# Threshold attention and a squared-ReLU layer on one core: another order of attention's steps, and chunk loads asked for earlier

## The chip, the cores and the metric

One Trainium2 chip, one of its cores. TensorE (PE) multiplies matrices, VectorE (DVE), ScalarE (ACT) and GpSimd (POOL) work element by element, and SyncE (SP) issues nearly all transfers of this kernel from one queue. Each engine takes its instructions in the order of its own queue and waits on semaphores for the others. The metric is the device time of one execution in microseconds (us), as the median of several runs.

## The reference

The inputs are q, k and v of 8 batches, 8 heads, 576 positions and 64 values per head, a threshold `tau`, and two weights, 512 x 2048 and 2048 x 512. Cut to what matters:

```python
scores = 1 / 8 * np.matmul(q, k.transpose(0, 1, 3, 2))
thresh = np.max(scores, axis=-1, keepdims=True) - tau
scores = np.where(scores >= thresh, scores, -1000000000.0)
scores = scores - np.max(scores, axis=-1, keepdims=True)
attn = np.exp(scores)
attn = attn / (np.sum(attn, axis=-1, keepdims=True) + 1e-09)
x = np.matmul(attn, v)              # then (B, H, S, D) -> (B*S, H*D): 4608 x 512
h = np.maximum(x @ w_in, 0.0)
out = (h * h @ w_out).astype(np.float32)
```

q, k, v and the output are 32-bit floats. The two weights come in as 64-bit floats, so the kernel reads them as pairs of 32-bit words and makes 32-bit floats of them with integer and float operations on the chip ("conversion").

## The kernel before

The kernel has two stages. Attention comes first and leaves its result, transposed, in the tensors `xT`; the two layers follow, each as products of 7 x 7 sums of blocks (a scheme with fewer products and more additions).

**Attention.** Two heads are a pair, 32 pairs in all. Rows of scores are worked in 144 units of 128 rows of two heads; two units, A and B, make a period, so there are 72 periods. For a unit: products of q and k into the PSUM tile `sc` (six banks, L448: `SA`, `SB` for 512 of the 576 columns, `RA`, `RB` for the rest of 64), a copy to SBUF that takes the row minimum of the scores, which are kept with their sign turned (`top`, L466, VectorE, one for each head), the threshold from the minimum (`least`, L473, POOL), the exponential (`pow`, L476, ScalarE), the mask, which multiplies by the comparison with the threshold and sums the row (`mask`, L481, VectorE). For the two units of a period: `over` (L488, POOL) adds 1e-9 to the row sums and `inv` (L491, VectorE) takes the reciprocal. The masked weights are then transposed by TensorE in three fills, `V`, `W`, `U` (L392), which are copied out by ScalarE as `eV`, `eW`, `eU` (L539). `V` and `U` use the one tile of the pool `pt` in turn, `W` uses banks 2 and 3 of `sc`, together with `Q` (L531), which spreads the reciprocals. `PV` (L548) multiplies by v into banks 0 and 5 of `sc`. `x` takes this out: the first head by a ScalarE copy (L679), the second by a VectorE product with the reciprocals (L681); `xm` (L691, POOL) scales the first head in SBUF. While weights are converted, ScalarE copies both heads and POOL scales both. `T` and `eT` (L412, L417, L425) turn q and k of a later pair through banks 1 and 4. A product must wait for every other engine that has touched its bank.

**The order.** It is written by hand. A period's list of names says in which order the steps are put into the queues; a name with dashes is the step of as many periods earlier:

```python
for name in BEGIN_WITH.get(p) or (CONVERTING if converts(p) else PLAIN):
    step(name.rstrip("-"), p - name.count("-"))
```

`CONVERTING` holds while weights are converted (periods 2 to 34), `PLAIN` after that; periods 0 and 1 have lists of their own. Nothing else ties the engines to a period: each runs on in its queue as far as its semaphores let it. A step that was already put in the queue by an earlier period isn't put in again.

**Weights.** The 16 blocks of the first weight and 16 blocks of the second are converted in attention, one chunk a period. `fetch` asks for a chunk's raw words (512 KB, L192) into one of four buffers `raw` of the region `cv`. `c1` (L206, ScalarE) makes a working tile `a`, one of four; `c2` (L213), `c3` (L220) run on POOL, `c4` (L228), `c5` (L236) on VectorE, and `c6` (L246, POOL) adds the parts into the tile `wall`, or, for the second weight, into `a`, which is then stored to HBM (L248). `c1` runs two periods after the `fetch`, `c6` two periods after `c1`. After the last conversion the steps `s1` and `s2` make one sum each of the first weight's blocks, and later of the first x, on POOL (L122 and L125); `s2` ends with period 59.

**Transfers.** `ahead(n)` issues up to n of the waiting loads of q and k (L296, L310, L317, L318; nine for a pair). `give_x` puts the stores of x (L594) in a list, and `ask` issues them; `valued` issues the loads of v (L327). All of these are in SP's queue, in the order in which the steps are called. `xm` calls `ask(False)` and `ahead(2)`, `ahead` at the head of a period issues three, and `c6` issues the store of its chunk at once.

Of the kernel before, what the change touches and what calls it, by code (L numbers as in the profile page):

```python
# [10 lines left out]
FP32 = mybir.dt.float32  # L11
# [37 lines left out]
def kernel(  # L49
# [88 lines left out]
    W_IN, W_OUT = {}, {}  # L138
    wall = ctx.enter_context(tc.tile_pool(name="wp", bufs=1)).tile([P, 49 * BANK], FP32, name="wall")

    def weight_tile(W, m, k):
        at = OUTER.index(m) * 7 + INNER.index(k)
        W[m, k] = wall[:, ds(at * BANK, BANK)]
        return W[m, k]
# [33 lines left out]
    def fetch(m):  # L178
        if m is None or m in asked_for:
            return  # L180
        asked_for.add(m)
        src = chunks[m][3]
        if not is_wide and m < 16:
            nc.sync.dma_start(out=weight(m)[:, :], in_=src)
            return
        raw = cv.tile([P, 2 * WC], I32, tag="raw", bufs=4, name="raw")
        if not is_wide:
            nc.sync.dma_start(out=raw[:, 0:WC].bitcast(FP32).rearrange("p (k o) -> p k o", k=4), in_=src)
            nc.sync.dma_start(out=slot_of(*chunks[m][1:3]), in_=raw[:, 0:WC].bitcast(FP32))
            return  # L190
        three = (lambda t: t.rearrange("p (k o) -> p k o", k=4)) if m >= 16 else (lambda t: t)
        nc.sync.dma_start(out=three(raw[:, :]), in_=src.bitcast(I32))  # L192
        raws[m] = raw
# [7 lines left out]
    def convert1(m):  # L201
        if m not in raws:
            return
        lo, hi = pick(raws[m], 0), pick(raws[m], 1)
        a = cv.tile([P, WC], I32, tag="a", bufs=4, name="a")
        nc.scalar.activation(out=a.bitcast(FP32), in_=hi.bitcast(FP32), func=AF.Abs)  # L206
        parts[m] = (lo, hi, a)
        raws.pop(m)
# [31 lines left out]
    def convert6(m):  # L240
        if m not in parts:
            return
        lo, hi, a = parts.pop(m)
        if m < 16:
            a = weight(m)[:, :].bitcast(I32)
        nc.gpsimd.tensor_tensor(out=a, in0=hi, in1=lo, op=ALU.add)  # L246
        if m >= 16:
            nc.sync.dma_start(out=slot_of(*chunks[m][1:3]), in_=a.bitcast(FP32))  # L248

    def sums(W, which, at):  # L250

# [353 lines left out]
    def begun(n):  # L605
        return starts.get(n)

    FIRST_PERIOD = -2
    PLAIN = """
        ahead PV-- RA- c2- c4- T- W-- U- c5- Q-- c1- maskB0-- x-- eT- SA- xm-- s1 maskB1-- RB- c3- eW-- SB-  # L610
        eU- topA0- V- powA0- eV- topA1- topB0- topB1- powA1- powB0- over- leastA- powB1- inv- c6 maskA0- s2-
        maskA1- leastB- fetch
    """.split()
    CONVERTING = """
        ahead SB- c1 RA topB0- powA1- c2- topB1- PV- c5- powA0- maskA0- eT- leastB- over- V- x- T powB0- SA
        RB W- maskA1- c3 c4 inv- Q- c6- fetch topA0 eV- topA1 leastA U xm- maskB0- powB1- eW- eU maskB1- s1
        s2
    """.split()

    BEGIN_WITH = {  # L620
        0: """
        SA RA RB SB fetch ahead topA0 T topA1 leastA topB0 topB1 leastB powA0 powA1 eT powB0 powB1 maskA0
        maskA1 maskB0 maskB1
        """.split(),
        1: """
        fetch ahead SA RA RB SB T eT over topA0 topA1 leastA inv V topB0 topB1 leastB powA0 powA1 eV W Q
        powB0 eW maskA0 maskA1 powB1 maskB0 maskB1 next
        """.split(),
    }

# [6 lines left out]
    def period(p):  # L637
# [34 lines left out]
        def values_out():  # L672
            if not has(2 * m):
                return
            late["x"] = x = sb.tile([P, 2, P], FP32, tag="x", bufs=2, name="x")
            for j in range(2):
                from_ = sc[:, ds(5 * j * BANK, P)]
                if converts(p) or j == 0:
                    made = nc.scalar.copy(x[:, j, :], from_)  # L679
                else:  # L680
                    made = nc.vector.tensor_tensor(  # L681
                        out=x[:, j, :], in0=from_, in1=wT[m][:, ts(SCALE_AT + j, P)], op=ALU.mult
                    )
                touch("x", made, 5 * j * BANK, P, m)

        def given_out():
            if has(2 * m):
                x = late.pop("x")
                made = x[:, 0 : 1 + converts(p), :].rearrange("p j n -> p (j n)")
                scale = wT[m][:, ds(SCALE_AT * P, (1 + converts(p)) * P)]  # L690
                nc.gpsimd.tensor_tensor(out=made, in0=made, in1=scale, op=ALU.mult)  # L691
                wT.pop(m)
                valued(m)
                give_x(m, x)
            ask(False)
            ahead(2)

        def scored(n):
            if has(n):
# [7 lines left out]
        def every(key):  # L707
# [10 lines left out]
            "c1": lambda: convert1(begun(p)), "c2": lambda: convert2(begun(p)),  # L718
            "c3": lambda: convert3(begun(p)), "c4": lambda: convert4(begun(p - 1)),
            "c5": lambda: convert5(begun(p - 1)), "c6": lambda: convert6(begun(p - 1)),  # L720
            "s1": lambda: sums_due(p) and sums_step(), "s2": lambda: sums_due(p) and p < 60 and sums_step(), "ahead": lambda: ahead(3 if p > 1 else 4),
            "fetch": lambda: fetch(begun(p + 2)),
            "next": lambda: fetch(begun(p + 3)),
        }
        steps["over"] = lambda: do(a, "over")
        steps["inv"] = lambda: do(a, "inverse")
# [654 lines left out]
```

## Time and profile before

| | |
|---|---|
| median of 3 runs | 1304.61 us (1299.85 to 1307.76) |
| the profiled execution | 1303.65 us, with a span of 1301.5 us |
| granted TensorE clock, mean | 0.995 |
| busy share of the span | PE 98%, PEld 86%, DVE 76%, POOL 76%, ACT 65% |
| SP's queue (q1) | 192.87 MB, 51.2% of the 16 DMA engines |

Times in the views count from the start of the span. PE is the matmuls, PEld their weight loads, SPq the issue of transfers by SP. A line number is that of the kernel before; a row gives the engine, the line, the operation, and what is written from what. "<-" names who ended the wait ahead of an instruction, inferred from semaphores. The ends of matmuls are modelled. Attention fills the first 512 us of the span: the first product of the layers begins at 512.11.

### The profile page before, as it was taken

The page shows a single profiled execution, that of the slowest core. Times are in us where ns is not written, and L with a number is a line of the kernel's source. Part 1 is how long each engine was busy: PE and PEld are TensorE (multiplying, and loading weights), DVE is VectorE, ACT ScalarE, POOL GpSimd, SP SyncE. Part 2 cuts the span into 40 slices and gives each one's busy share as a digit, 9 for nine tenths or more (in the row PEclk, how much of TensorE's full clock was granted, in tenths as well). Part 3 has the DMA queues.
Part 4 walks back from the last instruction along what each step waited for, and adds up shares of the span by engine and source line. Part 5 has one row for each costly group of instructions (what it writes and reads, how often), then busy time and mean ns, then how long its engine had stood idle before and what let it go on. Part 6 is the DMA issues. An engine that isn't in the chain of part 4 may idle for free.

```text
span 1301.5 us, 46003 instructions
## 1 busy us (share of the span) xinstructions
PE 1275.3 (98%) x18287; PEld 1118.3 (86%) x18287; DVE 989.4 (76%) x2384; ACT 847.9 (65%) x1537; POOL 989.4 (76%) x1070
## 2 busy tenths in 40 slices
PE   7999999999999999999999999999999999999998
PEld 4777767777777777988888888999999999999998
DVE  5999999999999995786886878867646654665463
ACT  5999989998898985566665866675523432343240
POOL 2999988877777531898987998868777767777775
PEclk8999999999999999999999999999999999999999
DMA  6565566544333312567768868679645224522511
GB/s 161 139 171 155 145 185 187 154 103 101 85 77 80 80 41 56 179 201 198 222 182 223 226 173 235 179 279 376 232 158 163 84 84 159 163 74 91 162 34 34
DMA packets 291414, 196.21 MB, mean 151 GB/s; under 512 B 100096, under 2 KB 252160, under 8 KB 291200
## 3 DMA queue, kind: packets, MB, share of 16 engines
q1 hardware_dynamic: 289888, 192.87, 51.2%
q8 instruction: 144, 2.36, 0.8%
q14 instruction: 70, 0.57, 0.1%
q10 hardware_dynamic: 1312, 0.41, 0.1%
HBM read 120.85 MB, written 72.35 MB: 148 GB/s over the span
## 4 chain that ended last, share of the span: by engine, by line
PE 83%; ACT 8%; DMA 3%; issue 2%; POOL 2%; SPq 1%; DVE 1%; ACTq 0%; DVEq 0%; POOLq 0%
PE po L1112 29%; PE ph L970 15%; PE sc L548 11%; PE sc L448 10%; PE ph L977 10%; PE pt L392 4%; ACT arena L539 3%; ACT arena L476 2%; PE sc L531 1%; PE sc L412 1%; DMA arena<-in_q_dram 1%; DVE arena L125 1%; POOL arena L125 1%; DMA arena<-xT 1%; ACT c L826 1%
## 5 line engine op out<-in xcount | busy, mean ns | idle before, releaser
L125 POOL TENSOR_TENSOR arena<-arena 128x512 f32<-128x512 f32 (+1 forms) x314 | 378.1, 1222 | 135.4 <-DVE arena L125 112.4
L1112 PE MATMUL po<-wall,arena 128*128 128x128 f32 x3528 | 394.7, 275 | 1.4 <-ACT arena L787 1.4
L1112 PEld LDWEIGHTS po<-wall,arena 128*128 128x128 f32 x3528 | 394.2, 192 | 1.8 <-ACT arena L787 1.8
L125 DVE TENSOR_TENSOR arena<-ph,arena 128x512 f32<-128x512 f32 x378 | 255.0, 688 | 79.8 <-PE ph L970 29.5
L122 POOL TENSOR_TENSOR arena<-arena 128x128 f32<-128x128 f32 (+1 forms) x322 | 270.0, 840 | 25.3 <-DMA arena<-w 9.4
L970 PE MATMUL ph<-arena,wall 128*128 128x256 f32 x1176 | 256.2, 380 | 1.9 <-DVE arena L125 1.6
L970 PEld LDWEIGHTS ph<-arena,wall 128*128 128x128 f32 x1176 | 222.3, 190 | 35.6 <-DVE arena L125 5.7
L125 DVE TENSOR_TENSOR arena<-po,arena 128x128 f32<-128x128 f32 x378 | 108.1, 289 | 168.6 <-PE po L1112 164.4
L476 ACT ACTIVATE arena<-arena 128x576 f32<-128x576 f32 x288 | 213.1, 779 | 24.2 <-DVE arena L466 24.2
L466 DVE TENSOR_SCALAR_CACHE_REDUCE arena<-sc 128x576 f32<-128x576 f32 x288 | 203.3, 752 | 31.5 <-issue 12.6
L481 DVE SCALAR_TENSOR_TENSOR arena<-arena 128x576 f32<-128x576 f32 x288 | 225.7, 820 | 1.3 <-ACT arena L476 1.3
L826 ACT COPY c<-arena 128x512 f32<-128x512 f32 (+1 forms) x295 | 169.0, 578 | 71.6 <-DVE arena L122 35.8
L448 PE MATMUL sc<-arena 64*64 64x512 f32 (+1 forms) x2304 | 191.8, 417 | 7.1 <-ACT arena L679 1.9
L548 PE MATMUL sc<-arena 64*64 64x128 f32 (+1 forms) x5760 | 164.7, 262 | 0.7 <-ACT arena L539 0.7
L122 DVE TENSOR_TENSOR arena<-arena,c 128x512 f32<-128x512 f32 x235 | 154.2, 665 | 11.0 <-ACT c L826 9.0
L548 PEld LDWEIGHTS sc<-arena 64*64 64x64 f32 x5760 | 149.9, 134 | 3.6 <-ACT arena L539 0.9
L539 ACT COPY arena<-pt 128x1024 f32<-128x1024 f32 x144 | 147.1, 1022 | 6.9 <-PE pt L392 6.3
L448 PEld LDWEIGHTS sc<-arena 64*64 64x64 f32 x2304 | 88.6, 134 | 73.1 <-issue 44.4
L473 POOL TENSOR_SCALAR arena<-arena,tau_p 128x2 f32<-128x2 f32 x144 | 84.7, 588 | 78.2 <-DVE arena L466 57.0
L787 ACT COPY arena<-po 128x128 f32<-128x128 f32 x63 | 16.6, 264 | 186.7 <-PE po L1112 183.9
L977 PE MATMUL ph<-arena,wall 128*128 128x128 f32 x1176 | 132.0, 275 | 0.6 <-DVE arena L681 0.6
L977 PEld LDWEIGHTS ph<-arena,wall 128*128 128x128 f32 x1176 | 131.6, 192 | 0.9 <-issue 0.7
(54 smaller groups left out, 1141.9 us busy)
## 6 DMA issues: line engine op xcount, KB each, us to landing
arena<-g SPq DMA_DIRECT2D x144, 256.0 KB, 4.5
g<-arena SPq DMA_DIRECT2D x192, 128.0 KB, 3.0
w<-arena SPq DMA_DIRECT2D x60, 256.0 KB, 2.8
wall<-w SPq DMA_DIRECT2D x49, 256.0 KB, 5.3
g<-arena SPq DMA_DIRECT2D x48, 256.0 KB, 3.7
arena<-w SPq DMA_DIRECT2D x44, 256.0 KB, 3.3
arena<-in_v_dram SPq DMA_DIRECT2D x32, 288.0 KB, 4.2
out_dram<-arena SPq DMA_DIRECT2D x70, 128.0 KB, 2.2
```

Of the source, the lines that this page charges most:

```text
L122: e.tensor_tensor(out=out, in0=x, in1=y, op=ALU.subtract)
L125: e.tensor_tensor(out=out, in0=x, in1=y, op=ALU.add)
L448: made = nc.tensor.matmul(sc[at, ds(to, count)], lhs, kT[rows, ds(at_k, count)], start=True, stop=True)
L466: made = nc.vector.tensor_scalar(out=s[:, j, :], in0=sc[:, ds(at, S)], scalar1=1.0, scalar2=None, op0=ALU.mult, op1=ALU.min, accum_out=nmx ...
L476: nc.scalar.activation(out=w[:, :, j, :], in_=of(j), func=AF.Exp, bias=nmx[:, j : j + 1], scale=-1.0)
L481: nc.vector.scalar_tensor_tensor(out=w[:, :, j, :], in0=of(j), scalar=thr[:, j : j + 1], in1=w[:, :, j, :], op0=ALU.is_le, op1=ALU.mult, a ...
L539: touch("weights", nc.scalar.copy(joined(to), whole(pt, 0, count)), at, 2 * BANK, m)
L548: made = nc.tensor.matmul(sc[ds(u * D, D), ds(5 * j * BANK + row, count)], loaded_v[i][rows, (c - (u != j)) % CH, :], wT[m][rows, ds(weigh ...
L826: nc.scalar.copy(c, y)
L970: nc.tensor.matmul(to[:, 2 * j : 2 * j + 2, :], W_IN[m, k][:, ts(2 * h + j, P)], part_x(steps, k, m), start=(not more and j == 0), stop=Tr ...
L977: nc.tensor.matmul(to[:, j, :], W_IN[m, k][:, ts(j, P)], x, start=(not more and j == 0), stop=True, skip_group_check=True,)
L1112: nc.tensor.matmul(to, g[:, j, :], w[:, j, :], start=(not more and j == 0), stop=(j == 3), skip_group_check=True)
```

## The change

Only attention's code is touched. The list for periods without conversions has another order, with some steps of an earlier period than before. In both lists the steps `put`, `give`, `fetch` and `ahead` stand together at the head: `put` issues the stores of chunks that `c6` has queued up to then, `give` the stores of x, `fetch` asks for the chunk that is used three periods later (and for the one two periods later, if it hasn't been asked for), `ahead` issues five loads. `c6` and `xm` no longer issue transfers, but for the loads of v. The raw words have seven buffers, in the last two of the seven rows of `wall`, which hold no block until the sums are made; `a` has six, and x three. The lists of periods 0 and 1 place `fetch` and `ahead` otherwise.

```diff
+    raw_places = Region(wall, OUTER.index(5) * 7 * BANK, 49 * BANK)
...
-        raw = cv.tile([P, 2 * WC], I32, tag="raw", bufs=4, name="raw")
+        raw = raw_places.tile([P, 2 * WC], I32, tag="raw", bufs=7, name="raw")
...
-        a = cv.tile([P, WC], I32, tag="a", bufs=4, name="a")
+        a = cv.tile([P, WC], I32, tag="a", bufs=6, name="a")
...
         if m >= 16:
-            nc.sync.dma_start(out=slot_of(*chunks[m][1:3]), in_=a.bitcast(FP32))
+            made_chunks.append((slot_of(*chunks[m][1:3]), a.bitcast(FP32)))
+
+    made_chunks = deque()
+
+    def put():
+
+        while made_chunks:
+            to, from_ = made_chunks.popleft()
+            nc.sync.dma_start(out=to, in_=from_)
...
     PLAIN = """
-        ahead PV-- RA- c2- c4- T- W-- U- c5- Q-- c1- maskB0-- x-- eT- SA- xm-- s1 maskB1-- RB- c3- eW-- SB-
-        eU- topA0- V- powA0- eV- topA1- topB0- topB1- powA1- powB0- over- leastA- powB1- inv- c6 maskA0- s2-
-        maskA1- leastB- fetch
+        put give fetch ahead eU-- powA0-- V-- powA1-- eV-- maskA1-- PV-- powB1-- c1- RA- powB0-- T--
+        maskA0-- U- W-- Q-- x-- c4- maskB1-- SA- eT-- RB- maskB0-- topA0- over- topA1- c2 s2 leastA- eW--
+        SB- topB0- s1- c5 c6 topB1- inv- leastB- xm-- c3
     """.split()
     CONVERTING = """
-        ahead SB- c1 RA topB0- powA1- c2- topB1- PV- c5- powA0- maskA0- eT- leastB- over- V- x- T powB0- SA
-        RB W- maskA1- c3 c4 inv- Q- c6- fetch topA0 eV- topA1 leastA U xm- maskB0- powB1- eW- eU maskB1- s1
-        s2
+        put give fetch ahead SB- c1 RA topB0- powA1- c2- topB1- PV- c5- powA0- maskA0- eT- leastB- over- V-
+        x- T powB0- SA RB W- maskA1- c3 c4 inv- Q- c6- topA0 eV- topA1 leastA U xm- maskB0- powB1- eW- eU
+        maskB1- s1 s2
     """.split()
     BEGIN_WITH = {
         0: """
-        SA RA RB SB fetch ahead topA0 T topA1 leastA topB0 topB1 leastB powA0 powA1 eT powB0 powB1 maskA0
+        fetch SA RA RB SB topA0 T ahead topA1 leastA topB0 topB1 leastB powA0 powA1 eT powB0 powB1 maskA0
         maskA1 maskB0 maskB1
         """.split(),
         1: """
-        fetch ahead SA RA RB SB T eT over topA0 topA1 leastA inv V topB0 topB1 leastB powA0 powA1 eV W Q
-        powB0 eW maskA0 maskA1 powB1 maskB0 maskB1 next
+        fetch ahead SA RA RB SB T ahead eT over topA0 topA1 leastA inv V topB0 topB1 leastB powA0 powA1 eV W
+        Q powB0 eW maskA0 maskA1 powB1 maskB0 maskB1
         """.split(),
     }
...
-            late["x"] = x = sb.tile([P, 2, P], FP32, tag="x", bufs=2, name="x")
+            late["x"] = x = sb.tile([P, 2, P], FP32, tag="x", bufs=3, name="x")
...
                 give_x(m, x)
-            ask(False)
-            ahead(2)
...
-            "s1": lambda: sums_due(p) and sums_step(), "s2": lambda: sums_due(p) and p < 60 and sums_step(), "ahead": lambda: ahead(3 if p > 1 else 4),
-            "fetch": lambda: fetch(begun(p + 2)),
-            "next": lambda: fetch(begun(p + 3)),
+            "s1": lambda: sums_due(p) and sums_step(), "s2": lambda: sums_due(p) and p < 60 and sums_step(), "ahead": lambda: ahead(5),
+            "fetch": lambda: (fetch(begun(p + 2)), fetch(begun(p + 3)) if p > 1 else None), "put": put, "give": lambda: ask(False),
```

## The prediction

> **What bounds the kernel now.** I read the page's chain of waits first, then the busy time by stretch around one line, then the timeline of one steady period, then the waits of the stage with conversions.
>
> ```profile
> PE 83%; ACT 8%; DMA 3%; issue 2%; POOL 2%; SPq 1%; DVE 1%; ACTq 0%; DVEq 0%; POOLq 0%
> ```
>
> ```profile
> core 0: us, DVE busy (x), PEclk, DMA share, GB/s
> 44.17:91.85 47.68, 1.11 (x7) 1.00 0.60 160
> 91.85:248.15 156.30, 3.48 (x22) 0.99 0.62 168
> 161.03:170.86 9.83, 0.16 (x1) 0.92 0.78 218
> 266.46:426.68 160.22, 4.15 (x24) 1.00 0.39 90
> 426.68:499.00 72.32, 1.90 (x11) 1.00 0.25 57
> ```
>
> The chain is mostly TensorE, but the change touches attention alone, so its stages must be read by themselves. The second view counts the reciprocal of the softmax sums, one in each period; every stretch starts and ends just ahead of one. Attention runs at four speeds: 47.68/7 = 6.81 us a period with conversions in a quiet stretch, 156.30/22 = 7.10 in the rest of the conversions (one period took 9.83), 160.22/24 = 6.68 without conversions, and 72.32/11 = 6.57 at the end, where POOL makes one weight sum a period instead of two.
>
> One period without conversions, in the timeline (start, length, engine, line; in brackets the idle time before and who ended it):
>
> ```profile
> 403.96 0.76 DVE L466 TENSOR_SCALAR_CACHE_REDUCE arena<-sc 128x576 f32<-128x576 f32 x1 [0.56 <-issue]
> ...
> 404.71 0.58 PEld L392 LDWEIGHTS pt<-ident,arena 64*128 64x128 f32 x16 [0.81 <-ACT arena L539]
> ...
> 404.76 0.78 ACT L476 ACTIVATE arena<-arena 128x576 f32<-128x576 f32 x1 [0.62 <-DVE arena L466]
> ...
> 405.50 0.29 POOL L473 TENSOR_SCALAR arena<-arena,tau_p 128x2 f32<-128x2 f32 x1 [0.64 <-DVE arena L466]
> 405.52 1.01 ACT L539 COPY arena<-pt 128x1024 f32<-128x1024 f32 x1
> ...
> 405.76 1.28 POOL L122 TENSOR_TENSOR arena<-arena 128x512 f32<-128x512 f32 x1
> ...
> 406.68 0.17 DVE L491 RECIPROCAL arena<-arena 128x4 f32<-128x4 f32 x1
> ...
> 407.01 0.80 POOL L473 TENSOR_SCALAR arena<-arena,tau_p 128x2 f32<-128x2 f32 x1
> ...
> 408.13 0.58 PEld L392 LDWEIGHTS pt<-ident,arena 64*128 64x128 f32 x16
> ...
> 408.32 0.81 DVE L481 SCALAR_TENSOR_TENSOR arena<-arena 128x576 f32<-128x576 f32 x1
> ...
> 409.05 2.39 PE L448 MATMUL sc<-arena 64*64 64x512 f32 x24
> ...
> 409.06 0.28 DVE L681 TENSOR_TENSOR arena<-sc,arena 128x128 f32<-128x128 f32 x1
> ...
> 409.26 0.80 DVE L481 SCALAR_TENSOR_TENSOR arena<-arena 128x576 f32<-128x576 f32 x1
> 409.37 0.61 ACT L539 COPY arena<-sc 128x512 f32<-128x512 f32 x1
> 409.39 0.30 PEld L448 LDWEIGHTS sc<-arena 64*64 64x64 f32 x6 [0.20 <-DVE arena L681]
> 409.41 1.79 POOL L122 TENSOR_TENSOR arena<-arena 128x512 f32<-128x512 f32 x1
> ...
> 409.84 1.06 ACT L539 COPY arena<-pt 128x1024 f32<-128x1024 f32 x1
> ...
> 410.63 0.76 DVE L466 TENSOR_SCALAR_CACHE_REDUCE arena<-sc 128x576 f32<-128x576 f32 x1 [0.56 <-issue]
> ...
> 411.29 0.23 POOL L488 TENSOR_SCALAR arena<-arena 128x4 f32<-128x4 f32 x1
> ...
> 411.38 0.33 PEld L392 LDWEIGHTS pt<-ident,arena 64*128 64x128 f32 x8 [0.81 <-ACT arena L539]
> ```
>
> VectorE idles 0.56 us ahead of its first row minimum (L466, 403.96 and 410.63); it is dense for 6.67 - 0.56 = 6.11. What holds it stands further up. The scores (L448) start at 409.05, but the half that writes the second head's bank can't start until VectorE has scaled the second head's output out of that bank (L681, 409.06 to 409.34): weight loads resume at 409.39, with that instruction named. From L681's end to the next row minimum is 410.63 - 409.34 = 1.29 us, in which VectorE has one mask (L481) left, 0.74 from start to start (408.32 to 409.06). The rest is the idle time. So the loop that sets the period is VectorE, L681, the second half of the scores, the scores' rests, VectorE. TensorE loses 409.39 - 409.05 = 0.34 us in it.
>
> **The order without conversions.** In each engine's own queue the change is smaller than the list of names suggests, since most names only turn round in the loop. What is left: L681 goes ahead of both masks of the second unit instead of between them; masks and exponentials swap heads; the copy eV goes behind a second exponential; the fills U and W swap; and POOL runs over, sum, leastA, sum, leastB, scaling of x, where one sum stood behind the scaling of x.
>
> Step by step. With L681 one mask earlier, two masks (1.48 us) cover the 1.29, and VectorE need not idle there. TensorE then starts both halves together: its period is 6.67 - 0.34 = 6.33. That is more than VectorE's 6.11, so TensorE becomes the limit. ScalarE is idle 0.62 ahead of 404.76, so it needs 6.05; its last copy (eU) ends at 410.90, 0.48 ahead of the next fill at 411.38. The copy eV ends at 406.53; one exponential (0.78) later it still ends 0.8 ahead of the fill U at 408.13, which reuses its buffer; beyond that cover it would cost TensorE one for one. The swap of U and W moves work within TensorE's queue, ahead of the sums' spread as before, and costs nothing. I take 6.35 for both kinds of period: 24 x (6.68 - 6.35) + 11 x (6.57 - 6.35) = 7.9 + 2.4 = 10.3 us gained. The smallest gain is none; a middle one is the time that the waits view gives to L681 alone, 7.2 us in 35 periods:
>
> ```profile
> PEld pt L392 <- ACT arena L539: 28.4, 35, 0.8
> ...
> PEld sc L448 <- DVE arena L681: 7.2, 26, 0.5
> ```
>
> I stay near 0.34, because the loads' wait leaves out the time in which the first half's loads went on alone. The largest gain is VectorE's own density: 35 x 0.56 = 19.6.
>
> The first of these rows seems to promise more: TensorE waits 0.8 us a period for the copy eU. But eU has ended 0.48 us earlier, and the fill starts as the scores' last product ends (409.05 + 2.39 = 411.44, an end that is modelled). I count that row as the drain of the scores and give nothing for it. If the releaser that the view names were the right one, the period could fall to VectorE's 6.11, the second rival. The Trainium skill, "TensorEngine Tiling (Array Packing)", section "Tiling Modes", says that a change of tiling mode drains the array; here scores use 64*64 tiles and fills 64*128. By that rule the 0.8 us stays whatever ScalarE does, against what the view's releaser says.
>
> **Chunks, buffers and stores.** The transfers are the same in number and size, and the conversions stay. What moves is SP's queue: the store of a finished chunk and the two or three stores of x go to the start of the next period, where POOL has mostly made them; the chunk load is asked for three periods ahead and, with seven buffers in the idle end of the weight tile, waits for no POOL addition; five loads of q and k follow in one place.
>
> ```profile
> SPq L594 <- POOL arena L691: 23.6, 17, 3.9
> SPq L192 <- POOL wall L246: 5.8, 6, 2.0
> ```
>
> ```profile
> ACT arena L206 <- DMA arena<-in_moe_w_out_dram: 2.5, 3, 1.7
> ```
>
> ```profile
> 157.44 2.13 SPq L296 DMA_DIRECT2D arena<-in_q_dram  x2
> ...
> 160.22 0.38 SPq L192 DMA_DIRECT2D arena<-in_moe_w_out_dram  x1
> ...
> 160.31 0.34 PE L412 MATMUL sc<-ident,arena 64*128 64x64 f32 x2 [0.37 <-DMA arena<-in_q_dram]
> ...
> 165.94 0.69 ACT L206 ACTIVATE arena<-arena 128x512 f32<-128x512 f32 x1 [1.74 <-DMA arena<-in_moe_w_out_dram]
> ```
>
> SP stands still 23.6 us behind x and 5.8 behind chunks, so loads come late. The chunk asked for at 160.22 is needed at 165.94, after a wait of 1.74 us; exponentials and row minima queue behind it, and that period is the one of 9.83, 3.0 over the quiet 6.81. q asked for at 157.44 is waited for at 160.31. All excess over the quiet pace is 156.30 - 22 x 6.81 = 6.5 us. With a lead of three periods (20 us instead of 5.7) the chunk's part goes; of the other 3.5 I give about half to late q and k: 4.5 us gained, between 0 and 6.5. The quiet pace stays: the change takes nothing off VectorE. SP still waits for the scaling of x once a period, with the chunk load and five loads behind it; their lead covers that (the first rival, if not). The later stores keep x and a chunk's working tile one period longer, which the third and the sixth buffer cover; without them the copies of x (L679, L681) would wait.
>
> The start may lose. A second chunk load in one place and one more now stand ahead of the last loads of the third pair's k.
>
> ```profile
> 19.77 1.26 SPq L310 DMA_DIRECT2D arena<-in_k_dram  x2
> ...
> 29.08 0.47 PE L412 MATMUL sc<-ident,arena 64*128 64x64 f32 x10
> ```
>
> ```profile
> arena<-in_moe_w_out_dram SPq DMA_DIRECT2D x16, 512.0 KB, 5.0
> ```
>
> ```profile
> 15.00:20.00 5.00, 1.77 (x44) 1.29 (x42) 5.00 (x16) 4.34 (x7) 1.32 (x3) 0.91 1.03 317
> ```
>
> Two chunks of 512 KB at 317 GB/s are 3.3 us. Those k loads were issued from 19.77 on and turned at 29.08; SP no longer waits in between, so I take 0.5 us lost, with bounds 3.3 lost and 1 gained.
>
> **Sum.** 10.3 + 4.5 - 0.5 = 14.3 us off the profiled execution's 1303.65, which is 1.0 under the median of the runs, 1304.61: 1289.4 by the profile, 1290 as a median. The layers behind attention are the same instructions.
>
> **Rivals.**
> - Slower, by late loads: chunk loads now go ahead of q and k in SP's queue. If q and k land as late as at 160.31, each turn (L412) waits for a chunk's passage, 512 KB at 317 GB/s = 1.65 us. TensorE has 6.81 - 6.33 = 0.48 to spare, so 1.2 us in each of the 29 converting periods, 34 us, less 10.3: 1328. It decides as soon as loads land behind their turn. For it: the wait at 160.31. Against it: loads are asked for more than a period ahead once SP doesn't stand still.
> - VectorE becomes dense, because TensorE did wait for eU: 19.6 + 6.5 gained, 1278.
> - POOL takes the place of L681. After the last mask it now runs over, sum, leastA, sum, leastB ahead of the masks of the second unit. VectorE reaches the first of these 409.06 - 403.96 = 5.10 us after its first minimum, less one mask, plus L681 (0.20 to the next mask): 4.56. As the rows have POOL, 0.23 + 1.28 + 0.29 + 1.79 + 0.80 = 4.39, just inside. With every piece at its long form, 0.23 + 1.79 + 0.80 + 1.79 + 0.80 = 5.41: 0.85 late, a period of 6.96 where there are two sums, 24 x 0.28 = 6.7 lost, 2.4 + 4.0 gained: 1304. The Trainium skill, "SBUF — State Buffer", section "SBUF: two separate sides", calls the port pair that the two engines share an exclusive lock, with the loser blocked fully. POOL's longer forms beside masks (1.79 and 0.80, against 1.28 and 0.29 beside minima) look like such blocking, which speaks for this rival; VectorE's mask at 409.26, beside a sum, lost nothing.
> - The order does nothing, as the copies of ScalarE hold the rests as late as L681 did: 4.0 gained, 1300.6 as a median.
>
> **Chances.** Forecast 0.60, with 1284 to 1297 of its own; dense VectorE 0.14; no effect of the order 0.10; POOL 0.08; late loads 0.08. The range 1278 to 1301 takes in the second and the fourth rival and leaves out 0.16. A measurement tells 0.5%, 6.5 us, from no change: faster is under 1298, so 0.60 + 0.14 and a little for a fourth rival with the conversions' whole excess: 0.75; same 0.16; slower 0.09.
>
> **What would show it.** Right: without conversions the reciprocals 6.3 to 6.4 apart in both stretches, no load of the scores released by L681, idle time ahead of the minima about 0.2; no chunk waited for, no period with conversions over 7.3. Wrong: masks that wait for leastB; turns that wait for q or k; periods still of 6.68, with another releaser ahead of the minima.

## The result, and the profile after

| kernel | runs | median, us | range, us | against before, 95% interval |
|---|---|---|---|---|
| before | 4 | 1302.74 | 1299.85 to 1307.76 | |
| changed | 4 | 1290.64 | 1288.24 to 1291.45 | 0.9900 (0.9864 to 0.9936) |
| before, timed again | 9 | 1300.97 | 1299.38 to 1304.05 | |
| changed, timed beside it | 5 | 1288.80 | 1288.07 to 1292.97 | 0.9911 (0.9895 to 0.9928) |

The change saves about 1%, some 12 us. The profiled execution of the changed kernel took 1288.24 us, with a span of 1286.1. In the changed kernel attention's lines have moved by about ten: the scores are L458, the fills L402, the row minimum L476, the mask L491, the reciprocal L501, the copies of the fills L549, the second head's scaling of x L691.

First the busy time by stretch around the reciprocal, of the changed kernel, with the same stretches as before the change (columns: window, its length, busy time and count of the reciprocals, granted clock, DMA share, GB/s). The second row has the rest of the conversions:

```profile
44.76:92.91 48.15, 1.11 (x7) 1.00 0.65 168
92.91:243.89 150.98, 3.48 (x22) 1.00 0.64 168
...
261.30:413.51 152.21, 4.15 (x24) 1.00 0.40 93
413.51:483.72 70.21, 1.91 (x11) 1.00 0.29 66
```

Periods without conversions now come every 152.21/24 = 6.34 and 70.21/11 = 6.38 us, where they took 6.68 and 6.57. The quiet converting periods take 48.15/7 = 6.88 (6.81 before), the rest 150.98/22 = 6.86 (7.10 before).

One period without conversions in the timeline of the changed kernel (start, length, engine, line, operation; in brackets the idle time before):

```profile
390.11 0.28 DVE L691 TENSOR_TENSOR arena<-sc,arena 128x128 f32<-128x128 f32 x1
...
390.31 0.81 DVE L491 SCALAR_TENSOR_TENSOR arena<-arena 128x576 f32<-128x576 f32 x1
...
390.83 2.03 PE L458 MATMUL sc<-arena 64*64 64x512 f32 x24
...
391.05 0.81 DVE L491 SCALAR_TENSOR_TENSOR arena<-arena 128x576 f32<-128x576 f32 x1
...
391.62 1.02 ACT L549 COPY arena<-pt 128x1024 f32<-128x1024 f32 x1
...
391.96 0.23 POOL L498 TENSOR_SCALAR arena<-arena 128x4 f32<-128x4 f32 x1 [1.46 <-DVE arena L491]
392.10 0.76 DVE L476 TENSOR_SCALAR_CACHE_REDUCE arena<-sc 128x576 f32<-128x576 f32 x1 [0.23 <-issue]
...
392.79 0.57 PEld L402 LDWEIGHTS pt<-ident,arena 64*128 64x128 f32 x16 [0.81 <-ACT arena L549]
...
394.81 0.17 DVE L501 RECIPROCAL arena<-arena 128x4 f32<-128x4 f32 x1
```

VectorE has done L691 (390.11 to 390.39) before the scores start at 390.83, so they run through in 2.03 us instead of 2.39. Two masks (390.31 and 391.05) now lie between L691 and the row minimum at 392.10, and VectorE idles 0.23 us there instead of 0.56. The fill at 392.79 starts as the scores end (390.83 + 2.03 = 392.86, modelled), 0.15 after the copy eU has ended (391.62 + 1.02 = 392.64).

The waits of both stretches without conversions (total us, times, longest) show the same:

```profile
POOL arena L498 <- DVE arena L491: 51.4, 35, 1.5
PEld pt L402 <- ACT arena L549: 28.4, 35, 0.8
...
PEld sc L458 <- ACT arena L427: 7.2, 26, 0.3
```

No row has loads of the scores released by L691 any more, where there were 7.2 us. The row of 28.4 us that names the copies of ScalarE stands unchanged to the tenth, though the period has become 0.3 us shorter. The loads' waits of 0.3 us at most for ScalarE's L427 come to 7.2 us as well, but they lie within the scores, which run through all the same in 2.03 us.

### The profile page after: what moved, and what is told of

It reads as the page before. It is cut to its first block, busy times and chain, and to the rows that moved or that the text cites. A ratio compares the mean times of both kernels' runs of the same rounds, so it can differ in the third digit from the quotient of the medians.

```text
span 1286.1 us, 45875 instructions
## 1 busy us (share of the span) xinstructions
PE 1259.6 (98%) x18287; PEld 1104.1 (86%) x18287; DVE 989.1 (77%) x2384; ACT 845.5 (66%) x1537; POOL 981.4 (76%) x1070
## 4 chain that ended last, share of the span: by engine, by line
PE 77%; ACT 13%; DMA 5%; issue 2%; DVE 1%; SPq 1%; POOL 0%; ACTq 0%; DVEq 0%; POOLq 0%
PE po L1119 29%; PE ph L977 16%; PE ph L984 8%; PE sc L558 8%; PE sc L458 7%; ACT arena L549 5%; ACT arena L486 4%; PE pt L402 4%; DMA wall<-w 2%; DMA arena<-xT 2%; PE sc L541 1%; PE sc L422 1%; ACT arena L208 1%; ACT arena L427 1%; ACT arena L435 1%
## 5 line engine op out<-in xcount | busy, mean ns | idle before, releaser
L122 POOL TENSOR_TENSOR arena<-arena 128x128 f32<-128x128 f32 (+1 forms) x322 | 265.1, 825 | 26.6 <-DMA arena<-w 10.6
L491 DVE SCALAR_TENSOR_TENSOR arena<-arena 128x576 f32<-128x576 f32 x288 | 226.0, 821 | 0.3 <-ACT arena L486 0.3
L476 DVE TENSOR_SCALAR_CACHE_REDUCE arena<-sc 128x576 f32<-128x576 f32 x288 | 203.3, 752 | 18.0 <-PE sc L458 6.2
L458 PE MATMUL sc<-arena 64*64 64x512 f32 (+1 forms) x2304 | 178.1, 413 | 5.9 <-ACT arena L549 1.7
L558 PEld LDWEIGHTS sc<-arena 64*64 64x64 f32 x5760 | 150.4, 133 | 4.4 <-ACT arena L549 0.9
L549 ACT COPY arena<-pt 128x1024 f32<-128x1024 f32 x144 | 145.8, 1013 | 7.1 <-PE pt L402 6.4
L458 PEld LDWEIGHTS sc<-arena 64*64 64x64 f32 x2304 | 76.7, 133 | 70.5 <-issue 46.0
L483 POOL TENSOR_SCALAR arena<-arena,tau_p 128x2 f32<-128x2 f32 x144 | 83.3, 578 | 57.7 <-DVE arena L476 44.4
```

What stands on the lines that cost most here:

```text
L122: e.tensor_tensor(out=out, in0=x, in1=y, op=ALU.subtract)
L458: made = nc.tensor.matmul(sc[at, ds(to, count)], lhs, kT[rows, ds(at_k, count)], start=True, stop=True)
L476: made = nc.vector.tensor_scalar(out=s[:, j, :], in0=sc[:, ds(at, S)], scalar1=1.0, scalar2=None, op0=ALU.mult, op1=ALU.min, accum_out=nmx ...
L491: nc.vector.scalar_tensor_tensor(out=w[:, :, j, :], in0=of(j), scalar=thr[:, j : j + 1], in1=w[:, :, j, :], op0=ALU.is_le, op1=ALU.mult, a ...
L549: touch("weights", nc.scalar.copy(joined(to), whole(pt, 0, count)), at, 2 * BANK, m)
L558: made = nc.tensor.matmul(sc[ds(u * D, D), ds(5 * j * BANK + row, count)], loaded_v[i][rows, (c - (u != j)) % CH, :], wT[m][rows, ds(weigh ...
```

## The experiments

Medians are of the timed runs; where a kernel was run once, the text says so, and its time is read with the scatter of some us that single runs of one kernel show.

**The new order alone.** The kernel before with the changed list for periods without conversions; buffers, loads and stores as before.

```diff
-        ahead PV-- RA- c2- c4- T- W-- U- c5- Q-- c1- maskB0-- x-- eT- SA- xm-- s1 maskB1-- RB- c3- eW-- SB-
-        eU- topA0- V- powA0- eV- topA1- topB0- topB1- powA1- powB0- over- leastA- powB1- inv- c6 maskA0- s2-
-        maskA1- leastB- fetch
+        ahead eU-- powA0-- V-- powA1-- eV-- maskA1-- PV-- powB1-- c1- RA- powB0-- T-- maskA0-- U- W-- Q--
+        x-- c4- maskB1-- SA- eT-- RB- maskB0-- topA0- over- topA1- c2 s2 leastA- eW-- SB- topB0- s1- c5 c6
+        topB1- inv- leastB- xm-- c3 fetch
```

> The kernel before with the new order for periods without conversions alone; buffers, loads and stores as before. Theory (the two gains are separate): periods without conversions of 6.34 us with two sums and 6.38 with one, as in the changed kernel; from the fourth to the 33rd reciprocal 204 us, as before; about 1292.5 us. Rival (the order needs the early transfers, since SP's waits for x now hold loads): periods of 6.5 or more, 1297 or more.

Measured: 1290.78 us (4 runs) against 1301.31 for before (13 runs), a ratio of 0.9906 (0.9869 to 0.9943). Its stretches by reciprocals, the one with all conversions first:

```profile
44.73:247.47 202.74, 4.58 (x29) 0.99 0.61 167
264.92:417.56 152.64, 4.15 (x24) 1.00 0.40 93
417.56:487.33 69.77, 1.90 (x11) 1.00 0.29 66
```

The periods are those of the changed kernel, 6.36 and 6.34, and so is the time. The order carries the gain.

**The transfers alone.** The changed kernel with the old list for periods without conversions (`put give fetch ahead` at its head, since these steps issue the transfers).

```diff
-        put give fetch ahead eU-- powA0-- V-- powA1-- eV-- maskA1-- PV-- powB1-- c1- RA- powB0-- T--
...
+        put give fetch ahead PV-- RA- c2- c4- T- W-- U- c5- Q-- c1- maskB0-- x-- eT- SA- xm-- s1 maskB1--
...
```

> The changed kernel with the old order for periods without conversions. Theory: from the fourth to the 33rd reciprocal 199 us (before 204.0, changed 199.1), the fourth reciprocal 0.6 us later than before, periods without conversions still 6.68 and 6.57; about 1298.5 us. Rival (late loads also slowed the periods without conversions): those periods shorter than 6.6, 1295 or less.

Measured: 1301.49 us (10 runs) against the same 1301.31: a ratio of 1.0001 (0.9981 to 1.0022). Stretches:

```profile
46.06:245.91 199.85, 4.57 (x29) 1.00 0.64 168
264.26:424.40 160.14, 4.15 (x24) 1.00 0.39 89
424.40:496.72 72.32, 1.90 (x11) 1.00 0.25 57
```

The periods without conversions are the old ones. The rival falls with them. The stretch with conversions is 4.1 us shorter than in the first profile of before (203.98), where 5 were forecast, but the fourth pair's reciprocal comes 1.9 us later (46.06 against 44.17) instead of 0.6, and the timed runs show no net gain: the median is 3 us above the expected 1298.5, a miss.

**The kernel before, once more**, for a second profile of it.

> The kernel before once more, for a second profile of its converting stretch (203.98 us between the fourth and the thirty-third pair in its first profile). Theory A (that stretch was long by chance of one execution, with its one period of 9.83 us at a low granted clock): 200 to 202 us, the plain periods 6.68 and 6.57 as they were, total about 1301. Theory B (the old transfers make it that long): 203.5 us or more again, about 1303.5.

Measured: 1305.31 us in one run. Its stretch with conversions, the long period in it, and the wait of ScalarE's first conversion (L206) for chunks between 44 and 250 us:

```profile
45.51:249.79 204.28, 4.61 (x29) 1.00 0.62 166
```

```profile
162.34:172.21 9.87, 0.16 (x1) 1.00 0.82 222
```

```profile
ACT arena L206 <- DMA arena<-in_moe_w_out_dram: 2.3, 2, 1.5
```

Theory A falls: the stretch is long again, and the period of 9.87 stands in the same place as the 9.83, now at a full clock, so the low clock of the first profile was not its cause. The timeline shows where 1.66 of its 3.1 us over the quiet pace come from:

```profile
161.67 0.38 SPq L192 DMA_DIRECT2D arena<-in_moe_w_out_dram  x1
...
167.10 0.69 ACT L206 ACTIVATE arena<-arena 128x512 f32<-128x512 f32 x1 [1.46 <-DMA arena<-in_moe_w_out_dram]
...
169.80 0.44 ACT L679 COPY arena<-sc 128x128 f32<-128x128 f32 x2
...
170.13 1.36 PE L448 MATMUL sc<-arena 64*64 64x512 f32 x16 [1.66 <-ACT arena L679]
```

The chunk asked for at 161.67 is waited for until 167.10; behind L206 on ScalarE stands the copy of x (L679, 169.80), and TensorE's scores wait 1.66 us for it.

**One name moved.** The kernel before, with only the second head's scaling of x ahead of the first mask of its unit.

```diff
-        ahead PV-- RA- c2- c4- T- W-- U- c5- Q-- c1- maskB0-- x-- eT- SA- xm-- s1 maskB1-- RB- c3- eW-- SB-
+        ahead PV-- RA- c2- c4- T- W-- U- c5- Q-- c1- x-- maskB0-- eT- SA- xm-- s1 maskB1-- RB- c3- eW-- SB-
```

> The kernel before with one name of the plain order moved: the second head's scaling of x ahead of the first mask; transfers as before. Theory (where this one instruction stands on VectorE decides the whole gain): plain periods 6.35 and 6.30 us instead of 6.68 and 6.57, 24 x 0.33 + 11 x 0.27 = 10.9 us off the median of before of 1301.3: 1290.4 us, the same as the changed kernel within 2 us. Rival (the freed time needs the changed transfers, or the other moves of the order): periods of 6.5 or more, 1295 us or more.

Measured: 1290.74 us (6 runs) against 1300.95 (11 runs), a ratio of 0.9912 (0.9892 to 0.9932). Stretches without conversions, then the loads of the scores in the waits of these stretches:

```profile
264.36:416.78 152.42, 4.13 (x24) 1.00 0.41 94
416.78:486.67 69.89, 1.88 (x11) 1.00 0.27 61
```

```profile
PEld sc L448 <- issue: 11.4, 42, 0.3
...
PEld sc L448 <- ACT arena L417: 7.8, 27, 0.5
```

6.35 us in both stretches: one name in a list of 42 gives the whole gain, and no load waits for L681. The other moves of the new order are worth nothing in time that these runs can tell. What they do is leave VectorE idle time: ahead of the row minima it waits 8.5 us in 35 periods of the changed kernel (5.4 and 3.1 in the waits view), and 1.8 here, at the same period. Here one mask of each period is held up by POOL's product of x, as it is in the run with L691 put back below.

**The same place with the changed transfers.** The changed kernel with the old list, `x--` moved ahead of `maskB0--` as above. One run:

> The changed kernel with the old order for periods without conversions, in which only the step x (ScalarE's and VectorE's part) is put ahead of the first mask of the second unit. Theory (VectorE's scaling of x was the wait, the rest of the new order is worth nothing): periods of 6.35 with two sums. Rival (the places of eV, the sums or the heads matter): 6.5 or more.

Measured: 1288.21 us, with periods of 152.56/24 = 6.36 and 69.22/11 = 6.29, as the theory had it. Since that was 2.4 us below the changed kernel's median, it was timed beside it:

> The changed kernel's transfers with the old plain order, in which only the second head's scaling of x stands one mask earlier (one look of it took 1288.2 us). Theory (that place gives the whole gain, the other moves of the order give nothing): 1290 to 1291 us, within 1.5 us of the changed kernel. Rival (the other moves of the order cost time, since one look was 2.4 us below the changed kernel's median): 1288 us.

> The changed kernel once more, on the same chip as the two kernels sent with it. Theory: 1290.6 us again, the plain periods 6.34 and 6.38 on average, the converting stretch 199 to 201 us and no wait of ScalarE's first conversion for a chunk.

Measured side by side: 1288.52 us (1287.04 to 1292.54) with only L691 moved, 1288.80 us for the changed kernel, ratios of 0.9906 (0.9890 to 0.9921) and 0.9911 (0.9895 to 0.9928). The 2.4 us were scatter; both came out below the expected 1290. The changed kernel's second profile has periods of 6.34 and 6.38 again and a stretch with conversions of 198.1. That a single profiled execution can stand some us off is plain from the changed kernel's own second profile:

```profile
core 0: 1290.8 us, clock 0.993
```

Against the first one, 1286.1 at 0.997, its fourth reciprocal came at 47.19 instead of 44.76, and it took 805.6 instead of 802.4 us behind its 71st reciprocal, with the same instructions.

**L691 back between the masks.** The changed kernel, with the one name put behind the first mask of its unit, where it stood before.

```diff
-        maskA0-- U- W-- Q-- x-- c4- maskB1-- SA- eT-- RB- maskB0-- topA0- over- topA1- c2 s2 leastA- eW--
+        maskA0-- U- W-- Q-- c4- maskB1-- x-- SA- eT-- RB- maskB0-- topA0- over- topA1- c2 s2 leastA- eW--
```

> The changed kernel with the step x put back between the two masks of the second unit, all else as changed. Theory: periods of 6.67 with two sums, idle time ahead of the row minima 0.5 to 0.6, loads of the scores released by the scaling of x. Rival (something else in the new order gives the gain): 6.45 or less.

Measured: 1305.76 us in one run, periods of 164.90/24 = 6.87 and 75.37/11 = 6.85. The rival falls. The whole gain is lost, and the periods are 0.2 us longer than the expected 6.67. Its waits without conversions, and one period:

```profile
PEld sc L458 <- DVE arena L691: 14.2, 33, 0.7
```

```profile
399.61 0.81 DVE L491 SCALAR_TENSOR_TENSOR arena<-arena 128x576 f32<-128x576 f32 x1
...
399.81 0.93 POOL L701 TENSOR_TENSOR arena<-arena 128x128 f32<-128x128 f32 x1
...
400.35 1.00 DVE L491 SCALAR_TENSOR_TENSOR arena<-arena 128x576 f32<-128x576 f32 x1
...
401.08 2.59 PE L458 MATMUL sc<-arena 64*64 64x512 f32 x24
...
401.28 0.28 DVE L691 TENSOR_TENSOR arena<-sc,arena 128x128 f32<-128x128 f32 x1
...
401.61 0.62 PEld L458 LDWEIGHTS sc<-arena 64*64 64x64 f32 x14 [0.39 <-DVE arena L691]
401.86 1.02 ACT L549 COPY arena<-pt 128x1024 f32<-128x1024 f32 x1
...
402.85 0.76 DVE L476 TENSOR_SCALAR_CACHE_REDUCE arena<-sc 128x576 f32<-128x576 f32 x1 [0.56 <-issue]
...
403.60 0.58 PEld L402 LDWEIGHTS pt<-ident,arena 64*128 64x128 f32 x16 [0.81 <-ACT arena L549]
```

The wait of the scores' loads for L691 is back, 14.2 us. From L691's end (401.56) to the row minimum (402.85) it is 1.29 us, the same 1.29 as before the change, and VectorE idles the same 0.56; 1.29 is the median of the 35 periods in both kernels. The extra 0.2 us is the mask at 400.35: it takes 1.00 instead of 0.81, with POOL's product of x (L701) still running when it starts and until 400.74, and L691 is behind it. 6.11 + 0.19 + 0.56 = 6.86, against 6.87 measured. A mask is held up by that product in each of the 35 periods.

**Less work for TensorE.** The changed kernel, with the product with v over seven of the nine blocks of keys; two are left out.

```diff
-        for c in range(CH):
+        for c in range(CH - 2):
...
-                            start=(c == 0 and s == 0), stop=(c == CH - 1), skip_group_check=True,
+                            start=(c == 0 and s == 0), stop=(c == CH - 3), skip_group_check=True,
```

> The changed kernel with the last two of the nine key blocks left out of the product of the weights with v; the scores, the exponentials and the masks are as they were. It takes about 0.49 us of TensorE's work out of each period, and it takes nothing from VectorE or ScalarE. Theory (TensorE's own work sets the plain period, and the product's second-half fill follows TensorE's drain of the scores): the plain periods fall from 6.34 until VectorE is dense, to 6.10 to 6.15 us; 35 plain periods give 7 to 8 us, the converting ones some more: 1278 to 1283 us. Rival (the chain scores, row minimum, exponential, transposition sets the period, not TensorE's work): periods of 6.30 to 6.35, 1288 us or little less.

Measured: 1284.07 us in one run, periods of 149.38/24 = 6.22 and 66.63/11 = 6.06. All engines in the two stretches (length, then busy time and count for PE, PEld, DVE, ACT, POOL):

```profile
261.59:410.97 149.38, 148.87 (x3716) 113.79 (x3711) 149.38 (x433) 142.32 (x246) 110.21 (x143) 1.00 0.41 96
410.97:477.60 66.63, 66.00 (x1690) 47.49 (x1686) 66.38 (x199) 63.99 (x109) 32.35 (x52) 1.00 0.30 69
```

The rival falls: the period does follow TensorE's work, and no load waits for L691 in this run either. It falls by 0.12 and 0.32 us and not by 0.49, since VectorE is now busy 149.38 of 149.38 us. (TensorE's modelled busy time tells nothing here: it was 232.53 of 232.53 us in both stretches before the change.) The forecast was missed, with 6.22 against 6.10 to 6.15 in the first stretch and a total above 1278 to 1283. 6.22 is 0.1 us above the 6.11 at which I had called VectorE dense, and one mask shows why:

```profile
298.26 1.28 POOL L122 TENSOR_TENSOR wall<-wall 128x512 f32<-128x512 f32 x1
...
299.08 1.07 DVE L491 SCALAR_TENSOR_TENSOR arena<-arena 128x576 f32<-128x576 f32 x1
...
300.08 0.81 DVE L491 SCALAR_TENSOR_TENSOR arena<-arena 128x576 f32<-128x576 f32 x1
```

The mask that starts at 299.08, while a sum of POOL runs until 299.54, takes 1.07 us; the next one takes 0.81. From start to start the first takes 1.00, where the same mask of the period read before the change took 0.81: 0.19 more. Against that, 6.11 had counted the last mask to its end, and back to back the next instruction starts 0.07 ahead of it (300.08 against 299.08 + 1.07): 6.11 + 0.19 - 0.07 = 6.23. In the second stretch, with one sum of POOL a period, the period is 6.06. The total is less far down than the periods say, since this run had 200.90 us with conversions, where no gain came, and 804.4 us behind its 71st reciprocal.

**Two questions on the transfers.** First the third period's chunk asked for from the sixth period on, then chunks asked for two periods ahead throughout.

```diff
-            "fetch": lambda: (fetch(begun(p + 2)), fetch(begun(p + 3)) if p > 1 else None), "put": put, "give": lambda: ask(False),
+            "fetch": lambda: (fetch(begun(p + 2)), fetch(begun(p + 3)) if p > 4 else None), "put": put, "give": lambda: ask(False),
```

> The changed kernel, but the fetch for three periods ahead begins at the sixth period instead of the third, so that the third pair's loads of keys stand behind fewer chunks. Theory (the start loses 0.6 us in the profile of the changed kernel because those loads wait behind two more chunks): the fourth pair's reciprocal at 44.2 instead of 44.8 us, all stages behind it as in the changed kernel: 1290.0 us. Rival (the start is set by the constants and the first transpositions alone): the same 44.8 us, 1290.6 us.

Measured: 1292.19 us (4 runs), a ratio of 0.9926 (0.9898 to 0.9954). The fourth pair's reciprocal stands at 46.07: a miss. The expected gain at the start did not come in this run. The views name another wait there than the third pair's k: that of TensorE's turns for q (`PEld sc L422 <- DMA arena<-in_q_dram`), at 20 to 23 us and, in some, once more near 30. In the eight profiles with the new transfers of the table below it comes to 1.1 us in the one with the fourth reciprocal at 44.14, to 2.0 to 3.5 in the three at 44.7 to 45.1, and to 4.3 to 4.8 in the four at 46.1 to 47.2. Why q lands so differently stays open.

```diff
-            "fetch": lambda: (fetch(begun(p + 2)), fetch(begun(p + 3)) if p > 1 else None), "put": put, "give": lambda: ask(False),
+            "fetch": lambda: (fetch(begun(p + 2)), None), "put": put, "give": lambda: ask(False),
```

> The changed kernel with the chunks' raw words asked for two periods ahead instead of three, the seven buffers and the later stores as they are. Theory A (asking earlier is what keeps ScalarE's first conversion from waiting for a chunk in the profiles): that wait is back, 1 to 3 us in the converting stretch, 201 to 203 us instead of 199.1; 1291 to 1293 us. Theory B (what keeps it from waiting is the later stores and the seventh buffer): no wait, 199 to 200.5 us, 1290.6 us.

Measured: 1289.29 us (4 runs), a ratio of 0.9904 (0.9888 to 0.9919). The stretch with conversions, and the longest wait for a transfer in it:

```profile
46.16:245.26 199.10, 4.58 (x29) 1.00 0.64 171
```

```profile
PEld sc L422 <- DMA arena<-in_q_dram: 0.5, 1, 0.5
```

No first conversion waits for a chunk in this stretch, and the stretch is as short as in the changed kernel. Theory B stands: asking three periods ahead is not needed; the seven buffers and the places of `put`, `give` and `fetch` do what there is to do. Which of these does it was not tried. In microseconds the load does go out earlier than before the change: from the sixth chunk on its issue is 7.5 to 11.2 us ahead of the conversion (15.6 to 19.0 in the changed kernel), where it was 4.4 to 9.3 before, and 5.7 for the chunk that was waited for at 165.94.

**All profiles together.** The four profiles with the old transfers and eight with the new ones (the one with fewer blocks of keys left out), worked out from the windows around the reciprocals of each profile:

| transfers | kernels | fourth reciprocal at, mean (range) | stretch with conversions, mean (range) |
|---|---|---|---|
| old | before twice, order alone, one name moved | 44.79 (44.17 to 45.51) | 203.1 (201.5 to 204.3) |
| new | changed twice, transfers alone, x first twice, x back, the two of the last part | 45.52 (44.14 to 47.19) | 199.4 (198.1 to 200.9) |

The ranges of the last column don't overlap: the new transfers save 3.7 us there. About 0.7 of it is lost at the start, where the ranges overlap widely.

## Why the prediction was right, point by point

- **What bounded the period.** Right, and confirmed by moving that one instruction both ways: L681 ahead gives 6.35, L691 back gives 6.87. The loop VectorE, L681, second half of the scores, VectorE is shown by the 1.29 us that come back with it. Of the signs that the prediction named for being right, the periods (6.34 and 6.38), the loads without L691, the idle time (0.23) and the chunks not waited for came; the last, no period with conversions over 7.3, did not: the changed kernel's profile has one of 7.4 and one of 8.17, its second one of 7.6.
- **The plain periods, 10.3 us.** Measured in the two profiles: 160.22 - 152.21 = 8.0 and 72.31 - 70.21 = 2.1, together 10.1. Another 0.9 comes from the three periods between the stretches (18.32 to 17.41 us), which the sum did not count. That TensorE's work sets the new period is shown by the run with less of it.
- **TensorE's 0.8 us ahead of the fill hang on the scores' end, not on the copy eU,** as the prediction had it. The row of the waits view named eU; the fill's loads start 0.07 us ahead of the modelled end of the scores in the changed kernel (392.79 against 392.86) and with L691 back (403.60 against 403.67), and 0.06 ahead, by the rounded rows, before (411.38 against 411.44), while eU ended 0.15, 0.72 and 0.48 us earlier. The lag behind the scores is fixed and the one behind eU is not: over all 35 periods the first is 0.07 in each of these kernels, and the second runs from 0.22 to 0.84 in the kernel before alone. With L691 back, the view names no releaser for 5 of the 35 waits of 0.8 us. So it isn't the copy; that it is the change of mode, and not any passage from scores to a fill, no run here separates. The rule of the Trainium skill, "TensorEngine Tiling (Array Packing)", section "Tiling Modes", that a change of tiling mode drains the array, agrees with these rows.
- **Dense VectorE (1278) did not come**, as that wait stayed. With less work for TensorE it comes, at 6.22 and not 6.11: the density was read from a period in which POOL held up no mask by more than 0.1 us, and counted the last mask to its end.
- **POOL in the place of L681 (1304) did not come.** The step `over` (L498) waits 1.46 us for VectorE's last mask at 391.96, 51.4 us in all: POOL is early. In the steady period both its sums start beside row minima and take 1.28, and of the two thresholds only the second (L483) takes its long form of 0.80. So POOL's run is 0.23 + 1.28 + 0.29 + 1.28 + 0.80 = 3.88 us, less than even the prediction's smaller sum (4.39), which had one sum of POOL in its long form. The threshold ends at 389.60 (388.80 + 0.80), 0.7 us ahead of the mask at 390.31. On the lock that this rival took from the Trainium skill, "SBUF — State Buffer", section "SBUF: two separate sides", the last section has what the masks show.
- **Late loads (1328) did not come.** SP still waits for the scaling of x, as foreseen, and little waits for SP:

```profile
SPq L604 <- POOL arena L701: 26.6, 20, 6.0
```

  Between 44 and 250 us the changed kernel's waits have no row for a DMA; its second profile has 0.2 us for q. The nearest to this rival is the kernel with fewer blocks of keys, where turns waited four times for q:

```profile
PEld sc L422 <- DMA arena<-in_q_dram: 4.0, 4, 1.9
```

- **Chunks and loads, 4.5 us, and the start, 0.5 us lost.** The mechanism was right in part. Between 44 and 250 us the wait of the first conversion for a chunk is in all four profiles with the old transfers (2.0 to 2.5 us) and in none with the new; at about 20 us three of the new ones have one of 0.3 to 0.5 us. The third period of lead that the prediction counts on isn't needed, by the run with two. The half of the other 3.5 us that it gave to late q and k isn't borne out: turns waited 0.5 and 0.6 us for q in two profiles with the old transfers and not in the other two, and up to 0.8 with the new. At the start the wait is for q, not for the third pair's k. And the size was off. The profiles give 3.7 less 0.7; the timed runs give a loss of 0.2 us for the transfers alone, with an interval from a gain of 2.5 us to a loss of 2.9 (0.9981 to 1.0022 of 1301.3). The term was worked out of one execution, which took 2.3 us more than the later median of the kernel (1303.65 against 1301.31). Whether executions without a profile have the late chunk as often stays open.
- **The sum.** 14.3 us were forecast, and about 12 came (1302.74 - 1290.64 and 1300.97 - 1288.80 are 12.1 and 12.2). The order gives 10 to 10.5 of it, by the two runs with old transfers (1301.31 - 1290.78 and 1300.95 - 1290.74). The rest is inside the scatter of medians. So the total came out near the forecast by its first term; the net 4.0 us of the others can't be told from nothing in the timed runs.

What is left in the stretch with conversions stays partly open. One period of 8.17 us, with full clock, stands in the changed kernel's profile from 208.71, and the same period of the order took 7.6 to 8.3 us in all eight profiles with the new transfers:

```profile
208.71:216.88 8.17, 0.16 (x1) 1.00 0.77 214
```

```profile
206.66 0.71 PE L402 MATMUL pt<-ident,arena 64*128 64x64 f32 x15
...
208.25 0.21 PE L402 MATMUL pt<-ident,arena 64*128 64x64 f32 x1 [0.89 <-issue]
...
208.56 1.01 ACT L549 COPY arena<-pt 128x1024 f32<-128x1024 f32 x1 [0.54 <-PE pt L402]
```

The fill of 16 stops after 15, and the last product stands 0.89 us with nothing that the profile shows to wait for; the copy waits behind it. In the changed kernel's second profile the same fill stops before the same product, for 0.30 us. The instructions of the program come in by transfers of their own (queue q8 in the page), which might explain it. That is not shown: the last packet of that queue had ended at 206.67 in the first profile and 208.29 in the second, ahead of both stops (from 207.37 and 209.37).

## What to carry to other kernels

When an engine idles at the same place in every period, go back along the loop to the instruction that gives the resource free, and see whether independent work stands in front of it in its queue; moving that one instruction gave all that a rewritten order gave. A releaser named by a view should be held against several periods and kernels: who ends at a fixed distance ahead is the releaser, who ends at changing distances is not. The price of a stall is read from more than one profile and then from timed runs, since what one execution lost in a stretch is not what the median loses.

## What the runs showed of the hardware

Of VectorE's masks and POOL's sums and products, the one that starts second is held up by the one that started first. The first mask of a period of the changed kernel, in its timeline:

```profile
387.54 1.28 POOL L122 TENSOR_TENSOR wall<-wall 128x512 f32<-128x512 f32 x1
...
388.55 0.89 DVE L491 SCALAR_TENSOR_TENSOR arena<-arena 128x576 f32<-128x576 f32 x1
```

The sum ends at 388.82, 0.27 us after the mask has started, and the mask takes 0.89. In the kernel with L691 back, 0.39 us of the product were left (400.74 against 400.35) and the mask took 1.00; with fewer blocks of keys, 0.46 us of the sum (299.54 against 299.08) and 1.07. Each is what POOL had left plus 0.61 or 0.62, where a mask that POOL doesn't hold up takes 0.80; so it is, to 0.01 us, for all 28 masks of the changed kernel's 35 periods that met a sum with more than 0.2 us left. The mask thus loses 0.18 to 0.19 us less than what POOL had left. The other way round, the sum at 409.41 in the kernel before starts 0.15 us behind the mask at 409.26 and takes 1.79 where it takes 1.28 beside row minima; that mask had its 0.80. By the Trainium skill, "SBUF — State Buffer", section "SBUF: two separate sides", a VectorE operation with two inputs in SBUF and a POOL operation that reads SBUF share ports: whichever starts first holds them for its whole instruction, and the other blocks. These rows agree: the masks have two inputs in SBUF, and the row minima, beside which the sums keep 1.28, read PSUM. The prediction read the mask at 409.26 as a sign against it; it was the one that had started first. VectorE's density therefore depends on where POOL's instructions begin, by up to 0.26 us a mask here (1.07 against 0.81).

The time behind the 71st reciprocal, nearly all of it the layers, was 805.6 us in one profile and 802.4 in another of the same kernel, at mean granted clocks of 0.993 and 0.997.
